# Sorted attention into a two-layer network: a longer run of products on zeros, values sorted around q's transposes, w_in's first half loaded in two steps, and the second half batch one slot earlier

## The chip, the cores and the metric

One core of a Trainium2 chip runs the kernel. Its engines work from their own instruction streams: PE (TensorE, matmuls and transposes, with weight loads shown as PEld), DVE (VectorE), ACT (ScalarE), POOL (GpSimd) and SP (SyncE). Loads that turn float32 into bfloat16 are issued by POOL. The metric is the time of one execution on the device in microseconds (us); the kernel before takes 233.49 us, the median of 8 runs (232.13 to 235.15).

## What is computed

The inputs are q, k, v of shape (batch 4, heads 8, sequence 768, head size 64), and for each batch and head an 8 x 8 matrix `sort_net`. The sequence is cut into 8 blocks of 96 rows.

```python
P = sort_net                        # (4, 8, 8, 8)
for _ in range(5):                  # Sinkhorn: rows, then columns
    P = exp(P - max(P, -1)); P = P / (sum(P, -1) + 1e-9); P = P / (sum(P, -2) + 1e-9)
k_sorted = einsum('bhij,bhjcd->bhicd', P, k_blocks)     # same for v
attn = softmax(q_block @ k_sorted_block.T / 8)          # inside each block of 96
x = attn @ v_sorted_block           # all heads side by side: (3072, 512)
h = x @ w_in                        # w_in (512, 2048)
out = (s * relu(h)**2 + b) @ w_out  # w_out (2048, 512) -> (3072, 512) float32
```

## The kernel before, in words

**Tiling.** A batch is worked on in two half batches of 4 blocks (384 rows of x), so there are 8 half batches. For one half batch, `ffn1` (line 366) computes h transposed, 128 of the 2048 columns at a time: 16 such chunks, two to a PSUM tile `hps`, so 8 pairs i = 0 to 7, each of 2 x 4 products of 384 columns (the four values of hp are the four groups of 128 rows of w_in). ACT applies the relu (line 392), DVE squares (line 393), and `ffn2` (line 397) multiplies the result by w_out, three groups of 128 rows with 16 products of 512 columns each.

**Attention pieces.** `k_piece` (239) and `v_piece` (277) sort 16 of the columns of k and v with 32 small products by a matrix `pd` built from P, and copy the PSUM tile on ACT ("A") or DVE ("D"). There are three key pieces (columns 0, CK, 2*CK) and four value pieces for a batch. The value pieces read `vp`, a copy of v in another order; POOL makes it for batches 1 to 3 with eight copies (`v_sort`, 473), and ACT for batch 0. `q_piece` (255) transposes q of half a batch on PE (16 transposes, tile `tq`, copied to `qt`). `s_piece` (290) makes scores for two heads of a half batch, with the exponential on ACT; `s_banks` (304) does the same in the two PSUM banks of another pool. `p_piece` (320) multiplies by v, and DVE divides by the sums (lines 336 and 337) into x. `t_piece` (342) transposes half of the columns of x into `xt`, which `ffn1` reads.

**Order.** The order is written out by hand: every engine follows its own instructions as they stand in the program. `psa` is a PSUM pool of three buffers used in turn by key, value, q, score, output pieces and `hps`; `psb` has two, for transposes of x, `s_banks` and `ffn2`. A piece waits for its buffer to be freed by the engine that copied the earlier content.

**The start.** While DVE and ACT run Sinkhorn (lines 174 to 196), PE runs products on zeros: `warm(n, w)` (146) issues n of w columns. Then come the pieces of batch 0's first half (lines 430 to 458). The three k loads and the first four q loads are issued early. `load_w` (125) is POOL's next work: it stands behind a small POOL copy that reads a key piece's result (line 437), so that it starts after that piece. It loads w_in in twelve DMAs: the first half of the columns for the four row groups a = 0 to 3 (256 KB each), then the third and the fourth quarter of the columns (128 KB each); q's second half (`load_q(0, range(HB, NB))`, four DMAs) goes behind the first four; w_out follows in four DMAs. After POOL's memsets come the loads of batch 1 (`loads(1)`, 483) and its eight copies `v_sort`. At most eight POOL loads are under way: each waits for the landing of the eighth before it.

**Slots.** `ffn1(t, slots, ahead)` takes a table of pieces to put behind pair i. With `ahead=3` the products of row groups 0 and 1 of the first three pairs (`part(i, (0, 1))`) are issued first, since `xt` comes in two halves; then the loop finishes each pair. The table's entry -1 stands before the last of those three. In the kernel before, `ffn1(0)` has the second half of x's transposes at -1, q's second half at 2, the second half batch's scores and outputs at 3 to 7. `ffn1(1)` has the second half of its transposes at -1. After that, `ffn2(0)` and `ffn2(1)` carry the sorting and attention of batch 1, and so on for the rest (lines 531 to 550).

Of the kernel before, what the change touches and what calls it, by code (L numbers as in the profile page):

```python
# [22 lines left out]
def kernel(  # L23
# [12 lines left out]
    nc = tc.nc  # L36

    B, H, S, D = q.shape
    NB = sort_net.shape[-1]
# [6 lines left out]
    HB = NB // 2  # L46
# [6 lines left out]
    CK = 16  # L53
# [39 lines left out]
    def load_q(b, ns=range(NB)):  # L93

        if b not in QTOK:
            QTOK[b] = rawp.tile([BLK, NB, H, D], BF, tag="rawq", name="qtok")
        qv = q[b].rearrange("h (n t) d -> t n h d", n=NB)
        for n in ns:
            nc.gpsimd.dma_start(out=QTOK[b][:, n], in_=qv[:, n])  # L99
# [25 lines left out]
    def load_w():  # L125
        wiv = moe_w_in.rearrange("(a p) f -> p a f", p=128)
        for c, (f0, f1) in enumerate(((0, 2), (2, 3), (3, 4))):
            cs = slice(f0 * (d_ff // 4), f1 * (d_ff // 4))
            for a in range(NHP):
                nc.gpsimd.dma_start(out=wi[:, a, cs], in_=wiv[:, a, cs])  # L130
            if c == 0:
                load_q(0, range(HB, NB))
        wov = moe_w_out.rearrange("(f p) n -> p f n", p=128)
        for c in range(4):
            fs = slice(c * (NF // 4), (c + 1) * (NF // 4))
            nc.gpsimd.dma_start(out=wo[:, fs, :], in_=wov[:, fs, :])
# [9 lines left out]
    def warm(n, w=512):  # L146
        for _ in range(n):
            if not Z:
                Z.append(psb.tile([128, 512], FP, tag="b", name="z"))
            nc.tensor.matmul(out=Z[0][:, 0:w], lhsT=zeros[:, 0:128], rhs=zeros[:, 0:w],  # L150
                             start=True, stop=True)


    def permute(eng, b, src, cs=slice(0, C2), ds=slice(0, D)):
# [4 lines left out]
        else:  # L159
# [14 lines left out]
    nc.vector.tensor_reduce(out=rstat, in_=sn, axis=AX.X, op=ALU.max)  # L174
    nc.vector.tensor_tensor(out=sn, in0=sn, in1=rstat.broadcast_to([BH, NB, NB]),
                            op=ALU.subtract)
    warm(140, 64)
    warm(16)
    for it in range(5):
        nc.scalar.activation(out=sn, in_=sn, func=AF.Exp)  # L180
        if it >= 1:
# [57 lines left out]
    def k_piece(b, c0, eng):  # L239
        src, mov, dst = RAW["k", b], PD[b], KS[b % 2]  # L240
        ps = psa.tile([128, CK, 2, NG], FP, tag="a", name="tp")
        for c in range(CK):
            for e in range(2):
                nc.tensor.matmul(out=ps[e * 64:(e + 1) * 64, c].rearrange("p z g -> p (z g)"),  # L244
                                 lhsT=src[:, c0 + c, :],
                                 rhs=mov[:, e].rearrange("p z g -> p (z g)"),
                                 start=True, stop=True)
        evac(eng, dst[:, :, :, c0:c0 + CK], ps.rearrange("p c z g -> p g z c"))
# [6 lines left out]
    def q_piece(b, half, eng):  # L255

        n0 = half * HB
        qt = q_tile(b)
        ps = psa.tile([128, 2, 1024], BF, tag="a", name="tq")
        for n in range(HB):  # L260
            for hp in range(NHP):
                c0 = (n % 2 * NHP + hp) * BLK
                nc.tensor.transpose(
                    out=ps[:, n // 2, c0:c0 + BLK],
                    in_=QTOK[b][:, n0 + n, 2 * hp:2 * hp + 2, :].rearrange("p h d -> p (h d)"),
                    identity=ident[0:BLK, 0:BLK])
        evac(eng, qt[:, n0:n0 + HB].rearrange("p (m n) a t -> p m (n a t)", m=2),
             ps[:, :, 0:2 * NHP * BLK])
# [8 lines left out]
    def v_piece(b, d0, eng):  # L277
        ps = psa.tile([128, CK, 2 * NG], FP, tag="a", name="tv")
        for d in range(CK):
            for z in range(2):  # L280
                nc.tensor.matmul(out=ps[z * GAP:(z + 1) * GAP, d, :],  # L281
                                 lhsT=VP[b % 2][:, d0 + d, :], rhs=PD[b][:, :, z, :],
                                 start=True, stop=True)
        evac(eng, VS[b % 2][:, :, d0:d0 + CK], ps[0:KR].rearrange("p d g -> p g d"))
# [5 lines left out]
    def s_piece(b, half, hp):  # L290
        g0 = hp * NB + half * HB
        sc = psa.tile([128, 2, 512], FP, tag="a", name="sc")
        for n in range(HB):
            for e in range(2):
                pr = slice(e * 64, (e + 1) * 64)
                nc.tensor.matmul(out=sc[:, e, n * BLK:(n + 1) * BLK],  # L296
                                 lhsT=KS[b % 2][pr, g0 + n].rearrange("p z c -> p (z c)"),
                                 rhs=QT[b][pr, half * HB + n, hp, :],
                                 start=True, stop=True)
        at = atp.tile([KR, 2, TG], BF, tag="at", name="at")  # L300
        nc.scalar.activation(out=at, in_=sc[0:KR, :, 0:TG], func=AF.Exp, scale=scale)  # L301
        AT[b, half, hp] = at
# [17 lines left out]
    def p_piece(b, half, hp):  # L320
        g0 = hp * NB + half * HB
        atf = AT.pop((b, half, hp)).rearrange("p e t -> p (e t)")
        if hp == 0:
            X[b, half] = xp.tile([BLK, HB, d_model], BF, tag="x", name="x")
        x = X[b, half]
        pv = psa.tile([128, 2, 512], FP, tag="a", name="pv")
        for e in range(2):
            for n in range(HB):
                c0 = (e * HB + n) * BLK
                m = 128 if c0 + 128 <= 2 * TG else BLK  # L330
                nc.tensor.matmul(out=pv[0:m, e, n * VW:(n + 1) * VW],  # L331
                                 lhsT=atf[:, c0:c0 + m], rhs=VS[b % 2][:, e * NG + g0 + n, :],
                                 start=True, stop=True)
        pvv = pv[0:BLK, :, 0:HB * VW].rearrange("p e (n w) -> p e n w", w=VW)
        rec = rtp.tile([BLK, 2, HB], FP, tag="rec", name="rec")
        nc.vector.reciprocal(out=rec, in_=pvv[:, :, :, D])  # L336
        nc.vector.tensor_tensor(  # L337
            out=x[:, :, hp * 128:(hp + 1) * 128].rearrange("p n (e d) -> p e n d", e=2),
            in0=pvv[:, :, :, 0:D],
            in1=rec.unsqueeze(3).broadcast_to([BLK, 2, HB, D]), op=ALU.mult)  # L340
# [25 lines left out]
    def ffn1(t, slots, ahead=0):  # L366

        gt = gtp.tile([128, NF, TG], BF, tag="gt", name="gt")
        GT[t] = gt
        xt = XT[t]  # L370
        H1 = {}

        def part(i, hpl):
            if i not in H1:
                H1[i] = psa.tile([128, 2, 512], FP, tag="a", name="hps")
            for f in range(2):
                for hp in hpl:
                    fc = (2 * i + f) * 128
                    nc.tensor.matmul(out=H1[i][:, f, 0:TG], lhsT=wi[:, hp, fc:fc + 128],  # L379
                                     rhs=xt[:, :, hp, :],  # L380
                                     start=(hp == 0), stop=(hp == NHP - 1))

        for i in range(ahead):
            if i == ahead - 1:
                for p in slots.get(-1, ()):
                    p()
            part(i, (0, 1))
        for i in range(NF // 2):
            part(i, (2, 3) if i < ahead else range(NHP))
            rt = rtp.tile([128, 2, TG], BF, tag="rt", name="rt")  # L390
            h = H1.pop(i)[:, :, 0:TG]
            nc.scalar.activation(out=rt, in_=h, func=AF.Relu)  # L392
            nc.vector.tensor_tensor(out=gt[:, 2 * i:2 * i + 2, :], in0=rt, in1=rt, op=ALU.mult)  # L393
            for p in slots.get(i, ()):
                p()
# [37 lines left out]
    nc.scalar.copy(out=PB, in_=pe)  # L433
    warm(3)
    k_piece(0, 0, "A")

    nc.gpsimd.tensor_copy(out=ones[:, 0:1], in_=KS[0][:, 0, 0, 0:1])
    load_w()
    k_piece(0, CK, "D")
    k_piece(0, 2 * CK, "A")  # L440
    q_piece(0, 0, "D")
    v_piece(0, 0, "A")
    v_piece(0, CK, "D")
    v_piece(0, 2 * CK, "A")
    v_piece(0, 3 * CK, "D")
    s_piece(0, 0, 0)
    s_piece(0, 0, 1)
    s_piece(0, 0, 2)
    p_piece(0, 0, 0)
    s_piece(0, 0, 3)  # L450
    warm(1)
    p_piece(0, 0, 1)
# [56 lines left out]
    def SB(b, h, i): return lambda: s_banks(b, h, i)  # L509
    def P(b, h, i): return lambda: p_piece(b, h, i)  # L510
    def TP(b, h, i, eng): return lambda: t_piece(b, h, i, eng)
    def TD(b, h): return lambda: t_dma(b, h)
    def PDB(b): return lambda: build_pd(b)
    def QP(b, h, eng): return lambda: q_piece(b, h, eng)


    ffn1(0, {-1: [TP(0, 0, 2, "D")], 2: [QP(0, 1, "D")], 3: [SB(0, 1, 0)], 4: [SB(0, 1, 1), P(0, 1, 0)],
             5: [SB(0, 1, 2), P(0, 1, 1)], 6: [SB(0, 1, 3), TP(0, 1, 0, "D"), P(0, 1, 2)],
             7: [P(0, 1, 3)]}, ahead=3)
    ffn1(1, {-1: [TP(0, 1, 2, "D")], 1: [lambda: take_p(1, B - 1, PB), PDB(1)], 4: [PDB(2)],  # L520
             3: [sum_w], 5: [PDB(3), make_bias]}, ahead=3)
    gate = const.tile([128, 1], BF)

# [57 lines left out]
```

## Time and profile before

| what | value |
|---|---|
| median of 8 runs | 233.49 us |
| profiled execution | 233.46 us, its span 231.7 us |
| PE busy | 221.0 us (95% of the span) |
| PEld busy | 132.4 us (57%) |
| DVE, ACT, POOL busy | 125.5, 98.8, 66.5 us |
| ffn1 products (line 379) | 512, 87.2 us busy |
| ffn2 products (line 403) | 368, 85.7 us busy |
| products on zeros (line 150) | 162, 11.7 us busy |
| loads by POOL (queue q0) | 30,288 packets, 12.85 MB |

The span is the time from the first to the last instruction of the program in the profile; the profiled execution's own time is 1.76 us longer. "Busy" on PE counts overlapping matmuls once. The chain of waits follows the work that ended last back to the start, and gives each stretch to an engine and a line; "issue" is time in which the engine waited for nothing that the profile shows. In the timeline, a row is a group of like instructions: start, length, engine, line, operation, output and inputs, and the idle time before it with what ended it. A windows row has the stretch, the sum, then busy time (and count) of PE and PEld, the granted clock of PE, the DMA share and GB/s.

### The profile page before, as it was taken

The page shows a single profiled execution, that of the slowest core. Times are in us where ns is not written, and L with a number is a line of the kernel's source. Part 1 is how long each engine was busy: PE and PEld are TensorE (multiplying, and loading weights), DVE is VectorE, ACT ScalarE, POOL GpSimd, SP SyncE. Part 2 cuts the span into 40 slices and gives each one's busy share as a digit, 9 for nine tenths or more (in the row PEclk, how much of TensorE's full clock was granted, in tenths as well). Part 3 has the DMA queues.
Part 4 walks back from the last instruction along what each step waited for, and adds up shares of the span by engine and source line. Part 5 has one row for each costly group of instructions (what it writes and reads, how often), then busy time and mean ns, then how long its engine had stood idle before and what let it go on. Part 6 is the DMA issues. An engine that isn't in the chain of part 4 may idle for free.

```text
span 231.7 us, 5857 instructions
## 1 busy us (share of the span) xinstructions
PE 221.0 (95%) x2572; PEld 132.4 (57%) x2572; DVE 125.5 (54%) x221; ACT 98.8 (43%) x127; POOL 66.5 (29%) x108
## 2 busy tenths in 40 slices
PE   7998699899999999999999999999999999999993
PEld 7585355555556556555756556655555556654453
DVE  6768155664456743469657544489556634441221
ACT  4967157366315315662533416646243235660000
POOL 8437697236800005656000008292000000000000
PEclk9999799999999999999999999999999999999999
DMA  5999999999912556999111466995114640001212
GB/s 193 225 73 146 180 179 206 157 200 126 151 63 75 37 149 127 209 154 145 48 48 48 113 161 106 191 136 113 50 48 69 138 113 3 0 1 45 95 45 91
DMA packets 53354, 25.82 MB, mean 111 GB/s; under 512 B 44880, under 2 KB 48208, under 8 KB 53328
## 3 DMA queue, kind: packets, MB, share of 16 engines
q0 software_dynamic: 30288, 12.85, 45.6%
q1 hardware_dynamic: 23040, 12.59, 23.0%
q8 instruction: 20, 0.33, 0.6%
q14 instruction: 6, 0.05, 0.1%
HBM read 27.27 MB, written 6.29 MB: 145 GB/s over the span
## 4 chain that ended last, share of the span: by engine, by line
PE 88%; DVE 4%; ACT 3%; issue 2%; DMA 1%
PE ops L403 35%; PE hps L379 35%; PE tv L281 4%; PE pv L331 4%; PE sc L296 3%; PE tp L244 2%; PE ops L416 2%; ACT rt L392 1%; PE tr L351 1%; DMA sn<-in_sort_net_dram 1%; PE z L150 1%; ACT sn L180 1%; DVE sn L187 0%; DVE gt L393 0%; DVE rstat L185 0%
## 5 line engine op out<-in xcount | busy, mean ns | idle before, releaser
L379 PE MATMUL hps<-xt,wi 128*128 128x384 bf16 x512 | 87.2, 329 | 0.9 <-ACT xt L233 0.9
L403 PE MATMUL ops<-wo,gt 128*128 128x512 bf16 x368 | 85.7, 380 | 0.0
L392 ACT ACTIVATE rt<-hps 128x768 bf16<-128x768 f32 x64 | 51.0, 811 | 59.6 <-PE hps L379 51.4
L393 DVE TENSOR_TENSOR gt<-rt 128x768 bf16<-128x768 bf16 x64 | 47.8, 753 | 42.8 <-ACT rt L392 41.8
L379 PEld LDWEIGHTS <-wi 128*128 128x128 bf16 x512 | 49.9, 99 | 35.1 <-issue 3.3
L403 PEld LDWEIGHTS <-gt 128*128 128x128 bf16 x368 | 33.6, 98 | 36.5
L424 DVE SCALAR_TENSOR_TENSOR ot<-ops,s_bc,bias 128x512 f32<-128x512 f32 (+1 forms) x25 | 18.2, 730 | 30.5 <-PE ops L403 28.2
L301 ACT ACTIVATE at<-sc 112x768 bf16<-112x768 f32 x28 | 21.0, 808 | 29.0 <-PE sc L296 29.0
L99 POOL DMA_DIRECT2D qtok<-in_q_dram x32 | 24.8, 790 | 20.7 <-DMA rawv<-in_v_dram 8.8
L337 DVE TENSOR_TENSOR x<-pv,rec 96x512 bf16<-96x512 f32 x32 | 22.0, 687 | 1.1
L160 POOL COPY vp<-rawv 128x384 bf16<-128x384 bf16 x24 | 19.5, 868 | 0.0
L235 DVE CAST vs<-tv 112x1024 bf16<-112x1024 f32 x11 | 13.2, 1222 | 9.9 <-PE tv L281 9.8
L527 POOL COPY gate<-gt 128x1 bf16<-128x1 bf16 x2 | 0.4, 190 | 57.9 <-DVE gt L393 57.9
L331 PEld LDWEIGHTS <-at 112*128 112x128 bf16 (+1 forms) x256 | 12.9, 101 | 6.5 <-issue 0.3
L331 PE MATMUL pv<-vs,at 112*128 112x66 bf16 (+1 forms) x256 | 13.9, 195 | 0.0
L150 PE MATMUL z<-zeros 128*128 128x64 bf16 (+1 forms) x162 | 11.7, 244 | 1.2 <-DVE zeros L102 1.2
L281 PEld LDWEIGHTS <-vp 128*64 128x64 bf16 x512 | 8.8, 113 | 2.7 <-issue 2.5
L150 PEld LDWEIGHTS <-zeros 128*128 128x128 bf16 x162 | 8.1, 116 | 3.1 <-DVE zeros L102 1.2
L281 PE MATMUL tv<-pd,vp 128*64 128x64 bf16 x512 | 9.7, 197 | 0.0
L233 ACT CAST ks<-tp 128x1024 bf16<-128x1024 f32 x8 | 8.0, 1018 | 3.8 <-PE tp L244 3.8
L336 DVE RECIPROCAL rec<-pv 96x8 f32<-96x8 f32 x32 | 6.4, 199 | 5.1 <-PE pv L331 5.1
L233 ACT CAST vs<-tv 112x1024 bf16<-112x1024 f32 x5 | 5.1, 1018 | 9.2 <-PE tv L281 9.1
(73 smaller groups left out, 105.6 us busy)
## 6 DMA issues: line engine op xcount, KB each, us to landing
out_dram<-ot SPq DMA_DIRECT2D x23, 256.0 KB, 2.0
qtok<-in_q_dram POOLq DMA_DIRECT2D x32, 96.0 KB, 9.5
rawk<-in_k_dram POOLq DMA_DIRECT2D x3, 768.0 KB, 6.7
rawv<-in_v_dram POOLq DMA_DIRECT2D x3, 768.0 KB, 10.5
wo<-in_moe_w_out_dram POOLq DMA_DIRECT2D x4, 512.0 KB, 10.5
v0f<-in_v_dram SPq DMA_DIRECT2D x4, 384.0 KB, 4.4
wi<-in_moe_w_in_dram POOLq DMA_DIRECT2D x4, 256.0 KB, 7.0
wi<-in_moe_w_in_dram POOLq DMA_DIRECT2D x8, 128.0 KB, 4.9
```

The source lines that it names most:

```text
L99: nc.gpsimd.dma_start(out=QTOK[b][:, n], in_=qv[:, n])
L150: nc.tensor.matmul(out=Z[0][:, 0:w], lhsT=zeros[:, 0:128], rhs=zeros[:, 0:w], start=True, stop=True)
L160: eng.tensor_copy(out=o, in_=i)
L281: nc.tensor.matmul(out=ps[z * GAP:(z + 1) * GAP, d, :], lhsT=VP[b % 2][:, d0 + d, :], rhs=PD[b][:, :, z, :], start=True, stop=True)
L301: nc.scalar.activation(out=at, in_=sc[0:KR, :, 0:TG], func=AF.Exp, scale=scale)
L331: nc.tensor.matmul(out=pv[0:m, e, n * VW:(n + 1) * VW], lhsT=atf[:, c0:c0 + m], rhs=VS[b % 2][:, e * NG + g0 + n, :], start=True, stop=True)
L337: nc.vector.tensor_tensor(out=x[:, :, hp * 128:(hp + 1) * 128].rearrange("p n (e d) -> p e n d", e=2), in0=pvv[:, :, :, 0:D], in1=rec.unsq ...
L379: nc.tensor.matmul(out=H1[i][:, f, 0:TG], lhsT=wi[:, hp, fc:fc + 128], rhs=xt[:, :, hp, :], start=(hp == 0), stop=(hp == NHP - 1))
L392: nc.scalar.activation(out=rt, in_=h, func=AF.Relu)
L393: nc.vector.tensor_tensor(out=gt[:, 2 * i:2 * i + 2, :], in0=rt, in1=rt, op=ALU.mult)
L403: nc.tensor.matmul(out=ops, lhsT=gt[:, f, m * 128:(m + 1) * 128], rhs=wo[:, f, :], start=(f == 0), stop=(f == NF - 1))
L424: nc.vector.scalar_tensor_tensor(out=ot[:, ns], in0=ops, scalar=s_bc, in1=BIAS[0][:, ns], op0=ALU.mult, op1=ALU.add)
```

## The change

1. Ahead of all else, 180 products on zeros of 64 columns instead of 140, and 10 of 512 instead of 16.
2. `load_w` and the small copy that gates it come behind the third key piece and read its result, instead of the first one's.
3. Two value pieces come before q's transposes, two behind; the first goes to DVE and the second to ACT (before: ACT, DVE). The first `p_piece` comes before the third `s_piece`.
4. Within w_in's first half, q's four loads move from behind row group 3 to between row groups 1 and 2.
5. `ffn1`'s table may have entries before each of the three early parts: -2 stands before the second, -1 before the third. In `ffn1(0)`, x's transposes move to -2, q's second half from 2 to -1, and the scores and outputs of the second half batch one slot up, with the transposes of its x at 6 ahead of the last output. In `ffn1(1)` the second half of x's transposes moves to -2.

```diff
             for a in range(NHP):
+                if c == 0 and a == 2:
+                    load_q(0, range(HB, NB))
                 nc.gpsimd.dma_start(out=wi[:, a, cs], in_=wiv[:, a, cs])
-            if c == 0:
-                load_q(0, range(HB, NB))
...
-    warm(140, 64)
-    warm(16)
+    warm(180, 64)
+    warm(10)
...
         for i in range(ahead):
-            if i == ahead - 1:
-                for p in slots.get(-1, ()):
-                    p()
+            for p in slots.get(i - ahead, ()):
+                p()
             part(i, (0, 1))
...
     k_piece(0, 0, "A")
-
-    nc.gpsimd.tensor_copy(out=ones[:, 0:1], in_=KS[0][:, 0, 0, 0:1])
-    load_w()
     k_piece(0, CK, "D")
     k_piece(0, 2 * CK, "A")
+
+    nc.gpsimd.tensor_copy(out=ones[:, 0:1], in_=KS[0][:, 0, 0, 2 * CK:2 * CK + 1])
+    load_w()
+    v_piece(0, 0, "D")
+    v_piece(0, CK, "A")
     q_piece(0, 0, "D")
-    v_piece(0, 0, "A")
-    v_piece(0, CK, "D")
     v_piece(0, 2 * CK, "A")
     v_piece(0, 3 * CK, "D")
     s_piece(0, 0, 0)
     s_piece(0, 0, 1)
+    p_piece(0, 0, 0)
     s_piece(0, 0, 2)
-    p_piece(0, 0, 0)
     s_piece(0, 0, 3)
...
-    ffn1(0, {-1: [TP(0, 0, 2, "D")], 2: [QP(0, 1, "D")], 3: [SB(0, 1, 0)], 4: [SB(0, 1, 1), P(0, 1, 0)],
-             5: [SB(0, 1, 2), P(0, 1, 1)], 6: [SB(0, 1, 3), TP(0, 1, 0, "D"), P(0, 1, 2)],
-             7: [P(0, 1, 3)]}, ahead=3)
-    ffn1(1, {-1: [TP(0, 1, 2, "D")], 1: [lambda: take_p(1, B - 1, PB), PDB(1)], 4: [PDB(2)],
+    ffn1(0, {-2: [TP(0, 0, 2, "D")], -1: [QP(0, 1, "D")],
+             2: [SB(0, 1, 0)], 3: [SB(0, 1, 1), P(0, 1, 0)], 4: [SB(0, 1, 2), P(0, 1, 1)],
+             5: [SB(0, 1, 3), P(0, 1, 2)], 6: [TP(0, 1, 0, "D"), P(0, 1, 3)]}, ahead=3)
+    ffn1(1, {-2: [TP(0, 1, 2, "D")], 1: [lambda: take_p(1, B - 1, PB), PDB(1)], 4: [PDB(2)],
              3: [sum_w], 5: [PDB(3), make_bias]}, ahead=3)
```

## The prediction

> **What bounds the kernel now.** I read three views in this order: the chain of waits (once over the last part, once over the first), then PE's and POOL's timelines, then the DMA packets in short windows. The chain first, because it says how long a saving has to survive:
>
> ```profile
> by line: PE ops L403 45.8%; PE hps L379 36.3%; PE tv L281 3.9%; PE pv L331 3.8%; PE sc L296 3.1%; PE tp L244 2.8%; PE ops L416 2.0%; DVE ot L424 0.3%; issue 0.0%
> ```
>
> This is the chain from 60 us to the end: PE and nothing else. The change does not touch this stretch, so what PE gains or loses by about 60 us arrives at the end unchanged, and the question is when PE gets to ffn2(0) and the sorting pieces in it. Over 14 to 60 us the same view shows the places where PE is not the bound:
>
> ```profile
> 22.37 0.26 PE tr L351 x5
> 22.64 1.94 issue
> 24.57 0.31 PE tr L351 x3
> 24.91 0.81 ACT xt L233
> 25.76 2.29 PE hps L379 x8
> ...
> 32.81 0.56 DVE gt L393
> 33.37 0.88 DVE qt L235
> 34.29 0.35 PE scb L311 x8
> ```
>
> Two things are to be seen. PE stands for 1.94 us in the middle of eight transposes whose data are there, and then the first eight ffn1 products take 2.29 us. The products' share in two windows tells why:
>
> ```profile
> 26.30:29.40 3.10, 2.66 (x9) 1.08 (x8) 0.50 1.43 198
> 86.40:107.00 20.60, 20.60 (x128) 12.31 (x126) 1.00 1.25 164
> ```
>
> (The number after the two busy columns is the granted clock.) After the gap PE runs at half clock for about 3.4 us; undisturbed, 128 products take 20.6 us, 0.16 us each.
>
> **The gap.** The page has 5,144 matmuls and weight loads on PE and this queue:
>
> ```profile
> q8 instruction: 20, 0.33, 0.6%
> ```
>
> 20 packets for 5,144 instructions: one packet per 257. In the windows from 15.7 to 22.1 us there is none, between 22.1 and 23.1 us there is one; PE stops at 22.64, after some 960 instructions, and goes on 1.5 us after that packet. The packets served while the load queue is idle come when PE is within some forty instructions of 193 + 256n; 961 is such a number (n = 3), and the block that starts there would have been asked for one block earlier, at 705, near 16.9 us. I read it as a fetch of instructions queued behind w_in's packets, which began at 16.5. The Trainium skill speaks against this: "DMA: Bandwidth & Descriptors" (DMA queue model, Arbitration) has each DMA engine take turns between queues packet by packet, so a fetch would wait for one packet, about 0.2 us here; and "Runtime: NRT & Kernel Launch" (Instruction fetch mechanics) states blocks of 256 instructions, which fits the 257, but calls the cost of crossing mostly hidden. By the skill the gap has another cause and may travel with the transposes; by the trace it belongs to a place in the instruction stream. I go by the trace; the skill's answer is a rival below.
>
> **Part 1, products on zeros.** 40 more of 64 columns, 6 fewer of 512. At 5.8 to 7.0 us 47 small ones run in 1.2 us, 0.026 each: +1.0 us. At 7.4 to 10.9 us about 16 wide ones run in 3.5 us, 0.22 each: -1.3 us. The group ends 0.3 us earlier, and PE waits there anyway (0.43 us, for DVE's sn at 11.36). Cost on the path: nothing; the cover is that wait, and even at the early rate (88 in 4.6 us, 0.052 each) it would be 0.4 us over it. But 34 more pairs move every block boundary 68 instructions up the program: 961 falls in s_piece(0,0,3), and 705 in the second value piece, about 16.1 us.
>
> **Part 2, the sorting order and load_w's start.** load_w is gated by the third key piece instead of the first:
>
> ```profile
> 13.88 2.02 ACT L233 CAST ks<-tp 128x1024 bf16<-128x1024 f32 x2 [1.07 <-PE tp L244]
> 15.04 0.19 POOL L437 COPY ones<-ks 128x1 bf16<-128x1 bf16 x1 [6.74 <-ACT ks L233]
> 15.51 2.18 POOL L130 DMA_DIRECT2D wi<-in_moe_w_in_dram  x4 [0.28 <-issue]
> ```
>
> The second ACT copy ends at 15.90 instead of 14.90: every POOL load starts **1.0 us later**, wi at 16.5 with first packets near 17.5. The fetch asked for at 16.1 then finds an idle queue. (The block before it may be short: served at 14.66, 1.1 us long; in the worst case it holds PE from 16.1 to 17.2. That 0 to 1.1 us is covered by part 3.) The rest, walked with the durations of before (ACT copy 1.02, DVE copy 1.22, q's copy 0.96, a piece of 32 products 0.62, three psa buffers in turn): values 0 and 1 at 14.95 and 15.66, q at 16.3 to 17.0, its copy until 18.2, values 2 and 3 at 17.1 and 17.75, scores 0 at 18.4 (was 18.33), last value copy 19.7 (was 19.57), first p_piece 19.75 (was 19.85), the second 21.2 since it now waits for the first one's buffer (was 20.97). x for the first transposes is ready at 22.57 (was 22.36). So the reorder itself costs 0.2 us. Without the gap xt is there at 22.57 + 0.35 + 0.85 = 23.8 (was 25.71).
>
> **Part 3, q ahead of w_in's third and fourth rows.** Landings before, by issue plus time to land of each: wi 19.9, 22.7, 23.9, 25.1; then q's four every 0.65 until 27.7. New: wi 20.9, 23.7, q until 26.3, wi 27.5 and **28.75** (25.15 + 1.0 + 4 x 0.65). So the first products can start at 23.85, but those of slots (2,3) wait until 28.75: this is what is late next. Behind it on PE, in order: part(0), t_piece (its x at 24.25), part(1) until 25.55; q's transposes, held for the last q load at 26.3; part(2), held for their copy on DVE (0.96, until 27.55; it takes the same buffer), until 28.25; then 28.75 + 12 products = **30.55** for the third group complete. Before: 31.66. The first stall of 1.94 us and the slow clock are therefore mostly eaten by this wait: 1.1 us remains.
>
> **Part 4, the half batch one slot up.** From 31.66 before, PE needed 32.37 us to the first value piece of batch 1 at 64.03. In that lie q's transposes (0.68, now done) and three waits, by PE's waits: scb for DVE's qt 0.5, tr for ACT's at 1.0, tr for DVE's x 0.4. With q's copy done at 27.55, and t_piece and p_piece a slot earlier than the products that hide them, these go: -2.6. New ones: score pair 2 wants the two psb banks that ACT frees at 32.3 (0.2), the last t_piece waits for x (0.3): +0.5. So 30.55 + 32.37 - 2.1 = **60.8**.
>
> **What PE meets there.** Value piece 2 of batch 1 needs six of POOL's eight copies:
>
> ```profile
> 55.60 6.98 POOL L160 COPY vp<-rawv 128x384 bf16<-128x384 bf16 x8
> 64.03 1.71 PE L281 MATMUL tv<-pd,vp 128*64 128x64 bf16 x96
> ```
>
> The sixth ended at 60.9; the loads are all 1.0 us later and stream without a pause from 27 us on, so 61.9. PE wants it at 60.8 + 1.1 = 61.9. The cover of 4.2 us is gone, and from here POOL holds back any larger gain. (w_out lands about 45.4, sum_w wants it at 46; 0.6 us to spare.)
>
> **Sum.** 64.03 - 60.8 = 3.2 us off the span of 231.7: 228.5. The profiled execution took 233.46, 1.76 more than its span, so 230.3; its time stands 0.03 below the median of 233.49.
>
> **Rivals.**
> - *The gap is not a late fetch and travels.* Then part(0) starts at about 25.7 at half clock: 1.3 + 0.65 + 1.3 us, q 0.9, its copy until 30.9, third group complete 33.6; first value piece 63.8 at best, **232.9**. For it: the skill's two rules. Against: a stop between two transposes of one tile.
> - *The clock falls again*, in the wait for q and w_in between 25.5 and 28.75. "TensorE: Matmul & The Clock Gate" (Part 1) halves it after an idle window of 3.4 us; before, it fell when PE had about 0.7 us of work in 3.4. Here it has 1.9, so I cost it at nothing; if it falls, 13 products at 0.32 instead of 0.16 and a slower start: +1.6, **231.9**.
> - *The loads stay slow: slower than before.* w_in's second 256 KB took 2.7 us to land after the first, the third and fourth 1.2. If 2.7 is the price of this stretch and not of a queue starting up, then q takes 4 x 1.4 and the last w_in piece lands at 34.9: third group 36.7, first value piece 67.0, end +3.0, **236.5**. It decides from a landing at 32.0 on. Against: k's three pieces at the start landed the same way, 2.2 and then 1.2 apart.
> - *A later block is late* in another place, for 1.5 to 2 us: about **232**.
>
> **How the numbers follow.** A run is told from no change at about 0.5%, 1.2 us. Chances: forecast 0.53 (229.1 to 231.3: POOL's copies allow up to 1 us more where the loads run better, buffers 1 less), the clock 0.09, a later block 0.09, travelling 0.13, slow loads 0.16. Leaving out slow loads and a little below, the range is 229.0 to 234.0. Faster by over 0.5% (below 232.3): forecast, clock and half of the later block, 0.69 with a little of the travelling one; within: 0.15; slower: 0.16.
>
> **What would show it.** Right: no issue gap on the transposes near 22.6, part(0) before 24.2, granted clock 1.0 from 24 to 30, the fourth wi load at 28.75, third group complete near 30.5, first value piece of batch 1 near 60.8 with a wait of at most 0.5 us for vp behind it, nothing else after 60. Wrong: an issue gap of over 1 us anywhere on PE before 60, wi's last first-half load after 30, a row at granted clock 0.5, or score pieces waiting for qt.

## The result, and the profile after

The changed kernel takes 230.79 us (median of 11 runs, 229.39 to 233.03) against 233.47 us before (32 runs): a ratio of 0.987 (95% interval 0.985 to 0.990), 1.3% faster. A second set of six runs gave 230.0 us and 0.988 (0.985 to 0.991). The ratios leave out executions in a slower state, here the one of 233.03 us, so they are not the plain quotient of the medians. The profiled execution took 230.54 us with a span of 228.8 us, 2.9 us less than before.

The chain of waits over the first part no longer has the stop among the transposes. PE's timeline of the changed kernel (start, length, engine, line, operation, idle time before it and what ended it):

```profile
16.52 0.35 PE L281 MATMUL tv<-pd,vp 128*64 128x64 bf16 x10 [0.29 <-issue]
...
22.90 0.56 PE L351 MATMUL tr<-ident,x 96*128 96x96 bf16 x8
24.34 0.81 PE L379 MATMUL hps<-xt,wi 128*128 128x384 bf16 x4 [0.89 <-ACT xt L233]
...
27.88 0.97 PE L379 MATMUL hps<-xt,wi 128*128 128x384 bf16 x5 [1.05 <-DVE qt L235]
29.12 1.96 PE L379 MATMUL hps<-xt,wi 128*128 128x384 bf16 x11 [0.27 <-DMA wi<-in_moe_w_in_dram]
31.01 0.34 PE L311 MATMUL scb<-qt,ks 64*128 64x96 bf16 x8
...
62.52 0.44 PE L281 MATMUL tv<-pd,vp 128*64 128x64 bf16 x16 [0.35 <-POOL vp L160]
```

The eight transposes run through at 22.90. What is late next is what the prediction named: q's copy on DVE (1.05 us), then w_in's fourth row group, then, at 62.52, POOL's copies of v, which begin 2.1 us later than before:

```profile
57.68 6.36 POOL L160 COPY vp<-rawv 128x384 bf16<-128x384 bf16 x8
```

The two DMA queues in the window from 17.5 to 18.6 us, in which w_in's first packets fall, and the granted clock over the first products:

```profile
q0 software_dynamic: 37, 0.08, 47.0%
q8 instruction: 1, 0.02, 9.5%
```

```profile
24.00:30.50 6.50, 3.98 (x22) 1.97 (x22) 1.00 1.33 190
```

The one instruction packet of that window begins at 17.61 us, 0.2 us ahead of the first load packet (before: 22.17, behind 5 us of them), and the clock stays at 1.00. From 60 us on the chain is PE again, but for POOL:

```profile
by line: PE ops L402 44.2%; PE hps L379 36.3%; PE pv L331 3.8%; PE tv L281 3.3%; PE sc L296 3.1%; PE ops L415 2.0%; PE tp L244 1.9%; POOL vp L160 1.8%; DVE ot L423 0.3%; issue 0.0%
```

### The profile page after: what moved, and what is told of

It reads as the page before. It is cut to its first block, busy times and chain, and to the rows that moved or that the text cites. A ratio compares the mean times of both kernels' runs of the same rounds, so it can differ in the third digit from the quotient of the medians.

```text
span 228.8 us, 5926 instructions
## 1 busy us (share of the span) xinstructions
PE 219.9 (96%) x2606; PEld 132.5 (58%) x2606; DVE 124.9 (55%) x221; ACT 98.9 (43%) x127; POOL 65.8 (29%) x108
## 4 chain that ended last, share of the span: by engine, by line
PE 77%; DMA 11%; POOL 8%; ACT 1%; issue 1%; DVE 0%; POOLq 0%
PE ops L402 33%; PE hps L379 27%; DMA rawv<-in_v_dram 8%; PE z L150 5%; DMA wi<-in_moe_w_in_dram 3%; PE pv L331 3%; PE tv L281 2%; PE sc L296 2%; POOL vp L160 2%; PE tp L244 2%; POOL qtok L99 2%; PE ops L415 2%; POOL wo L136 1%; POOL wi L132 1%; ACT ks L233 1%
## 5 line engine op out<-in xcount | busy, mean ns | idle before, releaser
L379 PE MATMUL hps<-xt,wi 128*128 128x384 bf16 x512 | 85.9, 326 | 2.2 <-DVE qt L235 1.0
L392 DVE TENSOR_TENSOR gt<-rt 128x768 bf16<-128x768 bf16 x64 | 47.2, 743 | 42.9 <-ACT rt L391 41.8
L379 PEld LDWEIGHTS <-wi 128*128 128x128 bf16 x512 | 49.4, 98 | 36.1 <-issue 3.1
L423 DVE SCALAR_TENSOR_TENSOR ot<-ops,s_bc,bias 128x512 f32<-128x512 f32 (+1 forms) x25 | 18.2, 730 | 30.9 <-PE ops L402 28.6
L160 POOL COPY vp<-rawv 128x384 bf16<-128x384 bf16 x24 | 18.9, 846 | 0.0
L150 PE MATMUL z<-zeros 128*128 128x64 bf16 (+1 forms) x196 | 12.2, 236 | 1.2 <-DVE zeros L102 1.2
L281 PE MATMUL tv<-pd,vp 128*64 128x64 bf16 x512 | 10.4, 197 | 0.9 <-POOL vp L160 0.4
L150 PEld LDWEIGHTS <-zeros 128*128 128x128 bf16 x196 | 9.3, 117 | 2.4 <-DVE zeros L102 1.2
```

What stands on the lines that cost most here:

```text
L160: eng.tensor_copy(out=o, in_=i)
L281: nc.tensor.matmul(out=ps[z * GAP:(z + 1) * GAP, d, :], lhsT=VP[b % 2][:, d0 + d, :], rhs=PD[b][:, :, z, :], start=True, stop=True)
L423: nc.vector.scalar_tensor_tensor(out=ot[:, ns], in0=ops, scalar=s_bc, in1=BIAS[0][:, ns], op0=ALU.mult, op1=ALU.add)
```

## The experiments

The theory: PE's stop before was an instruction block that arrived late because it stood behind load packets. Such a stop belongs to a count of PE instructions, near 961, and to the time at which the block is asked for. The main rival: it has another cause and goes with the transposes. Parts are numbered here as in the prediction: part 1 is item 1 of the change, part 2 items 2 and 3, part 3 item 4, part 4 item 5.

### Ten products on zeros fewer, and nothing else

```diff
-    warm(140, 64)
+    warm(130, 64)
```

> The kernel before with 130 products on zeros of 64 columns instead of 140, nothing else. Theory (the 1.94 us gap is a late block of PE's instructions, so it sits at an instruction count, near 961, and not at the transposes): 20 instructions fewer ahead put that count behind the eight transposes, into the first ffn1 products. PE finishes the transposes near 22.9 us, x is copied by 23.8, the block that arrived at 24.6 before is there in time or nearly so (gap under 1 us, in line 379), no half clock. Then the third group of products is complete near 28 us instead of 31.7, and the end comes 2 to 3.5 us earlier: 230.0 to 231.5 us. Rival (the gap has another cause and stays with the transposes): gap of about 1.9 us at line 351 near 22.6 again, half clock behind it, 233.5 us.

The kernel takes 230.53 us, ratio 0.987 (0.984 to 0.991): **leaving out ten small products on zeros gains as much as the whole change.** PE's timeline of this kernel:

```profile
16.52 0.34 PE L263 MATMUL tq<-ident,qtok 96*128 96x96 bf16 x4 [0.29 <-DMA qtok<-in_q_dram]
...
23.19 0.56 PE L351 MATMUL tr<-ident,x 96*128 96x96 bf16 x8
24.64 1.46 PE L379 MATMUL hps<-xt,wi 128*128 128x384 bf16 x8 [0.89 <-ACT xt L233]
25.93 0.51 PE L351 MATMUL tr<-ident,x 96*128 96x96 bf16 x8
26.27 2.92 PE L379 MATMUL hps<-xt,wi 128*128 128x384 bf16 x16
```

No stop and no half clock: count 961 now lies in the first ffn1 products, which PE reaches after 24.6 us, and the packet that came at 22.3 was in place by then. In this execution q's first loads landed late, so that the value pieces began at 16.79 us instead of 15.81; without that 1.0 us the third group, complete at 29.0, would be near 28.0, and the block only just in time. That the profile shows no stop is therefore in part luck, but all six runs lie between 229.71 and 230.77 at a granted clock of 0.997 or more. The rival falls: no transposes, no wait and no load were changed in the program.

### The gate of the loads alone

```diff
     k_piece(0, 0, "A")
-    nc.gpsimd.tensor_copy(out=ones[:, 0:1], in_=KS[0][:, 0, 0, 0:1])
-    load_w()
     k_piece(0, CK, "D")
     k_piece(0, 2 * CK, "A")
+    nc.gpsimd.tensor_copy(out=ones[:, 0:1], in_=KS[0][:, 0, 0, 2 * CK:2 * CK + 1])
+    load_w()
     q_piece(0, 0, "D")
```

> The kernel before with only the gate of the weight loads moved behind the third key piece. Theory (the fetch is late because load packets stand before it): the loads start 1.0 us later, first packets near 17.5 us, after the fetch is asked for near 16.9; the fetch is served by 18, no gap at the transposes, first ffn1 product near 23.8 at full clock. The fourth w_in load lands near 26.1, the third group is complete near 28.2. From there POOL's copies for batch 1, 1.0 us later than before, hold value piece 2 near 61.9: end about 3 us earlier, 230.5 us. Rival (the gap stays with the transposes whatever the queue does): gap as before, and since the loads are later too, 233.5 to 234.

The kernel takes 230.93 us, ratio 0.989 (0.986 to 0.993). With the zeros of before, holding back the loads is enough too (w_in's first is issued at 16.34 us instead of 15.51):

```profile
21.93 0.56 PE L351 MATMUL tr<-ident,x 96*128 96x96 bf16 x8
23.37 1.54 PE L379 MATMUL hps<-xt,wi 128*128 128x384 bf16 x8 [0.89 <-ACT xt L233]
24.74 0.51 PE L351 MATMUL tr<-ident,x 96*128 96x96 bf16 x8
25.09 1.14 PE L379 MATMUL hps<-xt,wi 128*128 128x384 bf16 x5
27.63 1.96 PE L379 MATMUL hps<-xt,wi 128*128 128x384 bf16 x11 [1.41 <-DMA wi<-in_moe_w_in_dram]
```

The packet was served at 19.5 us, not by 18 as expected, but in time for count 961: PE could go on some 2.5 us later, near 22.0, and comes to 961 at about 22.2. In place of the stop came a wait of 1.41 us for w_in's fourth load, which landed at 27.6 and not at 26.1.

### The changed kernel with the gate of before

```diff
-    nc.gpsimd.tensor_copy(out=ones[:, 0:1], in_=KS[0][:, 0, 0, 2 * CK:2 * CK + 1])
+    nc.gpsimd.tensor_copy(out=ones[:, 0:1], in_=KS[0][:, 0, 0, 0:1])
```

> The changed kernel with the gate of the weight loads put back to the first key piece's result, all else as changed. Theory: the load packets begin at 16.5 us again, at about the time at which the block at count 961 is asked for (705, 16.0 to 16.5 us), so the fetch waits until about 22 us and PE stops at count 961, now in the fourth score piece near 20.9 us, until about 24.5; half clock behind it; x late by 3 us, end 232 to 234 us. Rival (no such fetch): no gap, all loads 1.0 us earlier, the wait for the fourth w_in load and for POOL's copies shorter by 1.0: 229.5 us.

The kernel takes 235.13 us, ratio 1.006 (1.003 to 1.010): slower than the kernel before, although the loads start 1.1 us earlier than in the changed kernel (15.46 instead of 16.56). PE's timeline and the windows (stretch, sum, busy time and count of PE, PEld, DVE, ACT, POOL, granted clock, DMA share, GB/s):

```profile
20.65 0.52 PE L296 MATMUL sc<-qt,ks 64*128 64x96 bf16 x13
24.45 0.31 PE L296 MATMUL sc<-qt,ks 64*128 64x96 bf16 x3 [3.27 <-issue]
```

```profile
24.20:28.00 3.80, 3.22 (x37) 2.58 (x38) 2.09 (x6) 0.81 (x1) 2.64 (x5) 0.50 1.22 203
28.00:34.00 6.00, 4.53 (x35) 2.94 (x33) 1.62 (x3) 0.80 (x1) 4.66 (x12) 0.59 0.99 145
```

The stop is in the score pieces, 3.27 us long, after some 960 PE instructions, with half clock from 22.7 to 32.9 us, three times 3.4 us. The packet was served at 21.9.

### Part 1 alone

```diff
-    warm(140, 64)
-    warm(16)
+    warm(180, 64)
+    warm(10)
```

> The kernel before with only part 1 (180 products of 64 columns, 10 of 512). The group on zeros ends 0.3 us earlier and costs nothing. Theory: count 961 moves 68 instructions up, into the fourth score piece near 20.4 us; the fetch is asked for near 16.4 us, just when the load packets begin, so it is a race: either it is served by 18 and there is no gap (then end near 230), or it waits until 22 and the gap is longer, from 20.4 to 24.5, not at the transposes (then 235 to 236). Rival: gap of 1.9 us at the transposes, 233.5.

The kernel takes 236.33 us, ratio 1.012 (1.008 to 1.016): by itself part 1 makes the kernel slower than before.

```profile
20.43 0.30 PE L296 MATMUL sc<-qt,ks 64*128 64x96 bf16 x6
24.13 0.26 PE L296 MATMUL sc<-qt,ks 64*128 64x96 bf16 x2 [3.40 <-issue]
```

The race between the fetch and the first load packets was lost: the packet was served at 21.7 us, and PE stops again after some 960 instructions, in what happens to stand there. Each of these four kernels has the stop where the count puts it, or has none because the block was there.

### The changed kernel without part 1

```diff
-    warm(180, 64)
-    warm(10)
+    warm(140, 64)
+    warm(16)
```

> The changed kernel without part 1 (140 products of 64 columns and 16 of 512 again). Theory (late block): count 961 now falls at the sixth of the first eight transposes, near 23 us, and the block is asked for near 17.2 us, just before the load packets begin at 17.5. If the fetch still gets ahead of them, nothing changes: 230.8 us. If not, PE stops at the transposes until about 25, but the wait for the fourth w_in load near 29 us covers it, and what is left is half clock behind it: 231 to 232 us. Either way the stop, if there is one, is at count 961. Rival (part 1 is worth something of itself, by a warmer clock): slower by 1 us or more without any stop at count 961, with a row of lower granted clock early.

The kernel takes 230.33 us, ratio 0.986 (0.981 to 0.991), not to be told from the changed kernel. Count 961 is back among the first transposes and shows as a small gap (the packet was served at 20.4):

```profile
22.32 0.34 PE L351 MATMUL tr<-ident,x 96*128 96x96 bf16 x4
22.90 0.33 PE L351 MATMUL tr<-ident,x 96*128 96x96 bf16 x4 [0.24 <-issue]
```

Part 1 gives the changed kernel nothing.

### The changed kernel without parts 3 and 4

q's four loads go behind w_in's fourth row group again, and both slot tables are those of before:

```diff
-                if c == 0 and a == 2:
-                    load_q(0, range(HB, NB))
                 nc.gpsimd.dma_start(out=wi[:, a, cs], in_=wiv[:, a, cs])
+            if c == 0:
+                load_q(0, range(HB, NB))
...
-    ffn1(0, {-2: [TP(0, 0, 2, "D")], -1: [QP(0, 1, "D")],
-             2: [SB(0, 1, 0)], 3: [SB(0, 1, 1), P(0, 1, 0)], 4: [SB(0, 1, 2), P(0, 1, 1)],
-             5: [SB(0, 1, 3), P(0, 1, 2)], 6: [TP(0, 1, 0, "D"), P(0, 1, 3)]}, ahead=3)
-    ffn1(1, {-2: [TP(0, 1, 2, "D")], 1: [lambda: take_p(1, B - 1, PB), PDB(1)], 4: [PDB(2)],
+    ffn1(0, {-1: [TP(0, 0, 2, "D")], 2: [QP(0, 1, "D")], 3: [SB(0, 1, 0)], 4: [SB(0, 1, 1), P(0, 1, 0)],
+             5: [SB(0, 1, 2), P(0, 1, 1)], 6: [SB(0, 1, 3), TP(0, 1, 0, "D"), P(0, 1, 2)],
+             7: [P(0, 1, 3)]}, ahead=3)
+    ffn1(1, {-1: [TP(0, 1, 2, "D")], 1: [lambda: take_p(1, B - 1, PB), PDB(1)], 4: [PDB(2)],
```

> The changed kernel without parts 3 and 4: q's loads behind all four w_in row groups again, and the two slot tables of before. Theory (the gain is the removed stop, and parts 3 and 4 only trade waits): the fourth w_in load lands near 26.5 us instead of 29.1, so the third group is complete near 28.4 instead of 31.0; q's transposes come at slot 2 near 29.2, behind q's last load; the waits of before in the second half batch (0.5 + 1.0 + 0.4 us) come back. First value piece of batch 1 near 60.7; end within 0.5 us of the changed kernel: 230.3 to 231.3 us. Rival (the slots are the gain): 2 us slower than the changed kernel, 232.8 us.

The kernel takes 230.89 us, ratio 0.990 (0.984 to 0.996); two of its six runs took 233.34 and 234.47 us, at a clock of 0.991 and 0.983, so it may lose a race too. In the profiled execution (230.43) the third group of products is complete near 28.8 us instead of 31.0, and then the waits of before are back (waits of PE, us in total, times, longest):

```profile
PE tr L351 <- ACT at L317: 1.0, 1, 1.0
...
PE scb L311 <- DVE qt L235: 0.5, 1, 0.5
...
PE tr L351 <- DVE x L337: 0.5, 1, 0.5
```

The first value piece of batch 1 comes at 61.16 (changed kernel: 60.43, and 0.35 of wait). Parts 3 and 4 trade one set of waits for another. The gain is part 2's, and in it the gate's, which brought as much alone.

### POOL's copies held back

Eight memsets of 128 columns on a tile that nothing reads, ahead of batch 1's copies, in the changed kernel:

```diff
         load_q(b)
+        if b == 1:
+            for _ in range(8):
+                nc.gpsimd.memset(pad, 0.0)
         v_sort(b)
```

> The changed kernel with eight small POOL memsets (about 2 us together, on memory that nothing reads) ahead of the eight copies for batch 1. Theory (from about 60 us POOL's copies set the end): value piece 2 waits about 2.3 us instead of 0.35, the end comes about 2.0 us later: 232.8 us. Rival (POOL's copies have slack and the profile's chain only touches them): 230.8 to 231.3 us.

In the profiled execution (231.75 us), PE now waits for POOL three times:

```profile
58.95 6.29 POOL L160 COPY vp<-rawv 128x384 bf16<-128x384 bf16 x8
...
62.19 0.44 PE L281 MATMUL tv<-pd,vp 128*64 128x64 bf16 x16 [0.33 <-POOL vp L160]
62.96 0.44 PE L281 MATMUL tv<-pd,vp 128*64 128x64 bf16 x16 [0.33 <-POOL vp L160]
63.74 0.44 PE L281 MATMUL tv<-pd,vp 128*64 128x64 bf16 x16 [0.34 <-POOL vp L160]
```

The copies began at 58.95 instead of 57.68, the last of these pieces at 63.74 instead of 62.52, and the span grew from 228.8 to 230.0: 1.3, 1.2 and 1.2 us. The expectation of 2.0 was too high because v's load landed 0.7 us earlier in this execution. PE came to these pieces at 60.85, only 0.4 us later than in the changed kernel, so it is the copies that hold them. In this execution, as in the changed kernel's, POOL's copies set the end, with no slack. The median over the 12 runs, 233.85 (0.1% above the kernel before), cannot show it: ten of them had a granted clock of 0.978 to 0.992, and even the profiled one has a stop of 0.81 us after some 960 instructions ("issue", in the fourth score piece), its packet served at 19.6. The race that part 2 means to win can still be lost. Why this kernel should lose it more often, with PE's instructions unchanged, stays open.

### A version with both

From the kernel before: 20 products on zeros fewer, x's transposes at -2 in both tables, q's transposes at slot 1, the second half batch one slot up, and value piece 2's share of batch 1's copies on ACT instead of POOL. Load order and gate are those of before.

```diff
-    warm(140, 64)
+    warm(120, 64)
...
+            if b == 1 and i in (4, 5):
+                continue
             permute(nc.gpsimd, b, RAW["v", b], ds=slice(i * 8, (i + 1) * 8))
...
+    ffn1(0, {-2: [TP(0, 0, 2, "D")], 1: [QP(0, 1, "D")],
+             2: [SB(0, 1, 0)], 3: [SB(0, 1, 1), P(0, 1, 0)], 4: [SB(0, 1, 2), P(0, 1, 1)],
+             5: [SB(0, 1, 3), P(0, 1, 2)], 6: [TP(0, 1, 0, "D"), P(0, 1, 3)]}, ahead=3)
...
+        if b == 0:
+            s0[3] = [lambda: permute(nc.scalar, 1, RAW["v", 1], ds=slice(32, 48))]
         ffn2(2 * b, s0)
```

> A version built on what the runs so far showed: the kernel before with 120 products of 64 columns instead of 140 (count 961 then falls into the first ffn1 products, where PE comes after its block has landed), load gate and load order of before, q's transposes at slot 1 and the second half batch one slot up as in the changed kernel, and two of POOL's eight copies for batch 1 (value piece 2's) done by ACT behind the key pieces. Theory: no stop, all loads 1.0 us earlier than in the changed kernel, third group complete near 28.3, first value piece of batch 1 near 58.8, no wait for POOL's copies: 228 to 229 us, about 2 us faster than the changed kernel. Rival (POOL's loads and copies set the end whatever PE does): not below 230 us.

**228.65 us** (228.22 to 229.17), ratio 0.979 (0.975 to 0.984): faster than both kernels. What each of its four edits gives was not measured apart.

```profile
24.50 2.77 PE L379 MATMUL hps<-xt,wi 128*128 128x384 bf16 x16
27.51 0.73 PE L263 MATMUL tq<-ident,qtok 96*128 96x96 bf16 x12 [0.25 <-ACT rt L391]
...
59.23 1.71 PE L281 MATMUL tv<-pd,vp 128*64 128x64 bf16 x96
```

The first value piece of batch 1 starts at 59.23 (expected 58.8; before 64.03) and its three pieces run without a wait.

### The changed kernel again, and its gate once more later

The changed kernel's first set had a wide spread. It was run once more, and beside it with the gate on the first value piece's copy:

> The changed kernel once more, to learn whether its spread (229.4 to 233.0 us) is a race between one fetch and the first load packets. Theory (race): the times fall into a group at 229.5 to 231 us with the granted clock at 1.0 over the span, and one at 231.5 to 233 with it below 0.995; a profile of the first group has no stop of PE at count 961, a profile of the second would have one in the fourth score piece near 21 us. Rival (spread of another origin): times evenly spread, clock not tied to them.

```diff
-    nc.gpsimd.tensor_copy(out=ones[:, 0:1], in_=KS[0][:, 0, 0, 2 * CK:2 * CK + 1])
-    load_w()
     v_piece(0, 0, "D")
+    nc.gpsimd.tensor_copy(out=ones[0:KR, 0:1], in_=VS[0][:, 0, 0:1])
+    load_w()
```

> The changed kernel with the gate of the weight loads on the first value piece's copy, 1.0 us later again. Theory (race): the load packets begin near 18.5 us, the fetch asked for near 16.5 is always ahead of them; no run shows a stop at 961 or a lower clock, the spread shrinks to about 1 us. All loads are 1.0 us later: the third group complete near 32.0 us, value piece 2 of batch 1 near 63.5: 231.3 to 231.9 us. Rival (the start of the loads doesn't matter to the spread): the same spread of 3 us or more, 1.0 us higher.

The changed kernel gave 229.32 to 230.61 with the clock at 1.0 in all six runs; in the first set the runs at 0.993 took 231.9 and 232.4 and the one at 0.985 took 233.0, but one at 1.0 took 231.3. That ties most of the spread to the clock; no profile shows an execution with the lower clock. The later gate gave 231.95 us, ratio 0.994 (0.992 to 0.997), a spread of 2.1 us, and here the theory missed: it expected a spread of 1 us and no lower clock, but five of the twelve runs have a granted clock of 0.993, among them the profiled one, which has no stop at 961.

```profile
28.08 0.52 PE L263 MATMUL tq<-ident,qtok 96*128 96x96 bf16 x8 [0.65 <-DMA qtok<-in_q_dram]
29.64 4.44 PE L379 MATMUL hps<-xt,wi 128*128 128x384 bf16 x16 [1.05 <-DVE qt L235]
```

16 products take 4.44 us instead of 2.76: the clock halved at 30.2 us, after the wait for q and its copy, not behind a late block. This is the prediction's second rival, and 0.65 us more of waiting ahead of q's copy than in the changed kernel was enough to bring it. Whether the changed kernel's slower runs come from this or from a lost race stays open.

## Why the prediction was right, point by point

- **The sum.** 230.3 us was forecast; the profiled execution took 230.54 and the median was 230.79. The mechanism held, but that the number is so close is partly luck: two errors, in parts 3 and 4, cancelled.
- **The bound.** Right: after the wait for POOL at 62.5 us the chain is PE's again, and the gain at the first value piece of batch 1 arrived at the end (behind the value pieces ffn2 goes on at 65.67 us before and at 62.90 after, 2.8 us; the span shrank by 2.9).
- **The gap.** Right, and now shown: four kernels move or remove the stop by changing only a count of zeros or the start of the loads. The reading from the trace held against the two rules of the Trainium skill that were set against it, one of which made the wait about 0.2 us: in the kernel before, PE is at count 705 at 17.05 us, the packet was served at 22.17. Why it waits so much longer than one packet no run shows. Two clauses were too sure. "Then finds an idle queue" was so in the profile by 0.2 us (served at 17.61), and not in the execution with the memsets (19.6). "Within some forty instructions" of 193 + 256n is up to 53 in the same profile.
- **Part 1.** "Cost on the path: nothing" holds in the changed kernel only. Alone it costs 1.2%, through the count and not through PE's work on zeros; in the changed kernel its worth is nothing too. That the block boundary moves was written down; that it makes part 1 the worst part by itself was not.
- **Part 2.** The loads came 1.0 us later as said (wi at 16.56). The reorder cost more than the stated 0.2: x was ready at 23.05, not 22.57. The second score piece waited 0.33 us for ACT, the first p_piece 0.46 for DVE, and the block that starts at 705 held PE 0.29 (bounds 0 to 1.1). All of it lay under the wait for w_in, as the step assumed.
- **Part 3.** The fourth w_in load was to land at 28.75 and landed at 29.07; the third group was to be complete at 30.55 and was at 30.97. The wait for q itself (until 26.3) did not come: q's last load landed at 25.68, before PE asked; its copy on DVE was the wait (1.05).
- **Part 4.** The rest to the first value piece was put at 30.3 us and took 29.5: neither of the two small new waits (0.5 together) showed up, and 0.3 more went. This error of 0.8 us more than cancelled part 3's of 0.4: PE was there at 60.43, forecast 60.8.
- **POOL.** The sixth copy was to end at 61.9 and ended at 62.48: v's load landed at 56.57, 2.1 us later than before and not 1.0. The wait of 0.35 us and the experiment with memsets show that it binds.
- **Rivals.** Travelling fell with ten zeros fewer. Slow loads did not come (fourth load at 29.07, far from 32.0). A stop in another place did not come in the profiled execution, but came, 0.81 us long, in the one with the memsets. The clock did not fall in the profiled execution but fell with the later gate, at a price of 1.7 us for 16 products where 1.6 was written: counting it at nothing was near the edge.

## What to carry to other kernels

Where the chain shows "issue" between two like instructions whose inputs are there, count the engine's instructions to that place before changing the work around it: if the page shows about one instruction packet for 256 instructions, as here, a few instructions more or fewer far ahead, or loads that begin a microsecond later, can move the stop to where nothing waits. Test an edit for that by adding or taking away instructions that compute nothing; otherwise its gain or loss may be credited to the wrong part. After a stop is gone, look at which copy or load stands at the next meeting point: here it was POOL's copies, which left nothing more to gain from PE alone.

## What the runs showed of the hardware that was not expected

- A 16 KB instruction packet waited for about 4 to 5.5 us behind load packets: in five kernels it was served at 21.7 to 22.9 us, and PE was at count 705 at 16.6 to 18.2. That it is asked for at 705 is inferred from the count, not recorded.
- PE went on 2.4 to 2.7 us after such a packet began, in every execution where it stood at a block's start: 22.17 to 24.57 in the kernel before, 14.09 to 16.52 in the changed one. A packet that is served ahead of the loads can thus still hold PE for some tenths.
- The stop's price is not its length: 3.4 us of stop with the zeros of part 1 alone cost 2.8 us more than the 1.94 us before, with half clock for 10.2 us (three stretches of 3.4) instead of 3.4.
- Half clock began after 3.41 us in which PE was busy for 0.77 us (before), 0.95 (part 1 alone), 1.23 (gate of before) and 1.72 (later gate, 1.02 of it transposes). In the kernel with the gate alone, a like stretch with 2.00 us, from 25.96 to 29.37, was not followed by half clock. No run was made to find the border between them, or what transposes count for.
